# One 64x64 burst for the next chunk's scores and this chunk's output, and state matmuls in bursts of their own

## The chip, the cores and the metric

The kernel runs on 1 core of one Trainium2 chip. The metric is device microseconds of one execution; most executions of one kernel agree within 0.3%. Comparisons are between executions with a granted TensorE clock of 0.99 or more.

## The reference, cut to what matters

Two attention layers on the same 2048 x 1024 input, each with 32 heads of 32 columns. A is linear attention, B looks at 8 earlier positions, two apart. A gate g mixes them.

```python
def _A_ref(x, wqkv, wo):                 # linear attention
    q, k, v = ...                        # x @ wqkv, split in heads
    pq, pk = phi(q), phi(k)
    kv  = einsum("bhsd,bhse->bhde", pk, v)        # the "state", 32 x 32 a head
    z   = einsum("bhsd->bhd", pk)
    num = einsum("bhqd,bhde->bhqe", pq, kv)
    den = einsum("bhqd,bhd->bhq", pq, z)[..., None] + 1e-6
    return (num / den) ... @ wo

def _B_ref(x, wqkv, wo):                 # window of W = 8 positions, dilation 2
    logits = einsum("bhsd,bhswd->bhsw", q, kg) * scale
    attn   = softmax(where(mask, logits, -1e9))
    return einsum("bhsw,bhswd->bhsd", attn, vg) ... @ wo

g = sigmoid((x * gate_w).sum(-1, keepdims=True))
return g * _A_ref(...) + (1 - g) * _B_ref(...)
```

## The kernel before

The work is nearly all dense 128x128 matmuls over 512 columns (the projections). Between them stand short bursts of small ones:

- **S**, scores of B for one chunk of queries: 32 matmuls on 64x64 tiles of the array;
- **PV**, the output of B for a chunk, token-major: 64 matmuls with 64 rows and 57 columns of weights, also on the 64x64 grid;
- **kv**, the state of A for two tiles of 128 tokens: 64 matmuls with 128 rows and 32 columns of weights.

There are 18 chunks and 16 token tiles. The four PSUM banks `SO` hold scores, and later the values of the same chunk; `main` has the other four, for dense groups and for the state. The first burst after all of these is called fold: it multiplies the state into A's output weights.

```python
def s_fn(e):                                     # S: 32 matmuls into all four SO banks
    for c in range(8):
        for h in range(2):
            for r in range(2):
                last = e.matmul(SO[2 * r + c // 4]..., kT[64 * r:..., c, ...], Q[64 * r:..., c, ...],
                                tile_position=(64 * r, 64 * h))
# ...
def rest(...):
    P.op("pe", s_fn, ..., writes=[s.iv for s in SO], name="S")        # a burst of its own
    # E = exp(scores) on ScalarE from the four SO banks, then the mask on VectorE
    def values():
        def each(e):                             # PV: 64 matmuls, back into the four SO banks
            for i in range(16):
                for w in range(2):
                    for h in range(2):
                        last = e.matmul(SO[2 * h + i // 8]..., E[64 * h:..., ...], vt[64 * h:..., ...],
                                        tile_position=(64 * h, 64 * w))
        fns = [each]
        if len(states) > 1 and states[1][0] <= slot_n[0]:
            fn, more, bank, add = state([states.pop(0)[1] for _ in range(2)])
            fns = fns + [fn]                     # kv of two token tiles behind the values
        P.op("pe", lambda e: [f(e) for f in fns][-1], ..., name="PV" if add is None else "PV+kv")
        # two reciprocals and two multiplies on VectorE, then the output's DMAs
    after(PVLAG, values)
# ...
def state(two):
    bank = main.next()
    def fn(e):                                   # kv: 8 x 2 x 4 matmuls, 128 rows x 32 columns
        for s in range(8):
            for i, (t, pkt, azt) in enumerate(two):
                for c in range(4):
                    last = e.matmul(bank.ap()[32 * c:32 * c + 32, ...], pkt[...], azt[:, h, :],
                                    start=(i == 0), stop=(i == len(two) - 1), tile_position=(0, 32 * c))
    def add():                                   # VectorE adds the bank to kva and so frees it
```

Of the kernel before, what the change touches and what calls it, by code (L numbers as in the profile page):

```python
# [7 lines left out]
ALU = mybir.AluOpType  # L8
AX = mybir.AxisListType
BF16 = mybir.dt.bfloat16  # L10
F32 = mybir.dt.float32
# [1105 lines left out]
def build_kernel(nc, A_x, A_wqkv, A_wo, B_x, B_wqkv, B_wo, gate_w, out):  # L1117
# [86 lines left out]
    ot = Ring([SB([128, 1024], BF16, "ot%d" % i) for i in range(2)])  # L1204
    rs = Ring([SB([128, 16], F32, "rs%d" % i) for i in range(4)])
    vr = Ring([SB([128, 33 * H], BF16, "v%d" % i) for i in range(2)])
# [22 lines left out]
    FILL = 0.2  # L1229
    PVLAG = 3  # L1230
    WARM = 11
    PASSES = 6
# [4 lines left out]
    def plan(seen):  # L1237
# [6 lines left out]
        class Pool:  # L1244
# [4 lines left out]

            def next(self):  # L1250
                if seen is None:
                    b = self.bs[self.n % len(self.bs)]
                else:
                    b = min((b for b in self.bs if b.take is None or b.take in P.read), key=lambda b: seen[b.take] if b.take is not None else -1.0)
                self.n += 1
                b.take = len(takes)
                takes.append(len(P.ops))
                return b

        for b in banks:  # L1260
            b.take = None

        def C(eng, fn, cost, writes, reads=()):
# [34 lines left out]
        def top_end(i, op):  # L1298
            P.op("dve", lambda e: e.tensor_reduce(mx4[:, i:i + 1], mx[i][:, :], AX.X, op), 0.15 + mx[i].row / 960.0, reads=[mx[i].all()], writes=[mx4.part((i, i + 1))])

# [117 lines left out]
        def fill(e_, qs, nq, offs):  # L1418
# [7 lines left out]

            Q, _ = qd.next()
            for k in range(2):
                src = qT[:, :, t0 + qs:t0 + qs + 2 * nq]
                fd = lambda e, k=k: e.tensor_scalar(Q[:, :, k, 0:2 * nq], src, par[:, k:k + 1], None, op0=ALU.mult)  # L1430
                fa = lambda e, k=k: e.activation(Q[:, :, k, 0:2 * nq], src, ACT.Copy, scale=par[:, k:k + 1])
                P.op("any", {"act": fa, "dve": fd}, {"act": act(16 * nq), "dve": 0.15 + 16 * nq / 1920.0}, reads=[qT.part((0, 8), (t0 + qs, t0 + qs + 2 * nq)), par.all()],
                     writes=[Q.part((0, 8), (k, k + 1), (0, 114))])

# [10 lines left out]
        def rest(e_, qs, nq, t0, k0, m, vt, Q, s_fn):  # L1445
            P.op("pe", s_fn, 0.46, mode="r", reads=[kT.part((0, 8), (t0 + k0[0], t0 + k0[1] + 64)), Q.all()], writes=[s.iv for s in SO], name="S")
            E, _ = Er.next()
# [3 lines left out]
            P.op("dve", lambda e: e.tensor_tensor(ev(), ev(), m[:, :, :].rearrange("p r q -> p (r q)")[:, None, :].to_broadcast([128, 16, 2 * nq]), ALU.mult),  # L1451
                 0.15 + 32 * nq / 1920.0, reads=[E.all(), m.all()], writes=[E.all()])

            def values():

                def each(e):
                    for i in range(16):
                        for w in range(2):
                            hd = 16 * w + i
                            for h in range(2):  # L1460
                                c = 33 * (i % 8)
                                g_ = place(hd)
                                last = e.matmul(SO[2 * h + i // 8].ap(c, c + 33)[64 * w:64 * w + nq, :], E[64 * h:64 * h + 64, g_ * nq:(g_ + 1) * nq],  # L1463
                                                vt[64 * h:64 * h + 64, hd * 33:hd * 33 + 33], start=True, stop=True, tile_position=(64 * h, 64 * w))
                    return last
                fns, rd, wr, add = [each], [vt.all(), E.all()], [s.iv for s in SO], None
                if len(states) > 1 and states[1][0] <= slot_n[0]:
                    fn, more, bank, add = state([states.pop(0)[1] for _ in range(2)])
                    fns, rd, wr = fns + [fn], rd + more, wr + [bank.iv]
                P.op("pe", lambda e: [f(e) for f in fns][-1], 0.55 + 0.5 * (len(fns) - 1), mode="c", reads=rd, writes=wr, name="PV" if add is None else "PV+kv")  # L1470
                if add is not None:
                    add()
                o, os_ = ot.next()
                for h in range(2):
                    r, _ = rs.next()
                    bv = lambda h=h: ps[:, 4 + 2 * h:6 + 2 * h, 0:264].rearrange("p k (i c) -> p k i c", c=33)
                    two = [SO[2 * h].iv, SO[2 * h + 1].iv]
                    P.op("dve", lambda e, r=r, bv=bv: e.reciprocal(r[:, :].rearrange("p (k i) -> p k i", k=2), bv()[:, :, :, 32:33].rearrange("p k i c -> p k (i c)")), 0.2,
                         reads=two, writes=[r.all()])
                    P.op("dve", lambda e, r=r, bv=bv, h=h: e.tensor_tensor(  # L1480
                        o[:, 512 * h:512 * h + 512].rearrange("p (k i c) -> p k i c", k=2, c=32), bv()[:, :, :, 0:32],
                        r[:, :].rearrange("p (k i) -> p k i", k=2)[:, :, :, None].to_broadcast([128, 2, 8, 32]), ALU.mult), dps(512),
                        reads=two + [r.all()], writes=[o.part((512 * h, 512 * h + 512))])
                q0 = t0 + qs
                for w, (r0, r1) in [(w, r_) for w in range(2) for r_ in ((0, 48), (48, nq))]:
                    P.op("sp", lambda e, w=w, r0=r0, r1=r1: e.dma_start(
                        oB_hbm[q0:q0 + 2 * nq, 512 * w:512 * w + 512].rearrange("(h q) f -> q h f", h=2)[r0:r1], o[64 * w + r0:64 * w + r1, :].rearrange("p (h f) -> p h f", h=2)), 0.5,
                        reads=[o.all()], writes=[[("O%d_%d" % (w, r0), q0, q0 + 2 * nq, None)]], chan="oo%d_%d_%d" % (os_, w, r0), lat=0.3)
                while rows[0] < NT and q0 + 2 * nq >= 128 * (rows[0] + 1):
                    t, rows[0] = rows[0], rows[0] + 1  # L1490
                    P.op("sp", lambda e, t=t: e.dma_start_transpose(qT[:, :, t * 128:(t + 1) * 128], oB_hbm[t * 128:(t + 1) * 128, :]), 1.5,
                         reads=[[("O%d_%d" % (w, r0), t * 128, (t + 1) * 128, None)] for w in range(2) for r0 in (0, 48)], writes=[qT.part((0, 8), (t * 128, (t + 1) * 128))], chan="ot%d" % t, lat=1.3)
            after(PVLAG, values)

        rows = [0]
        pace = [0.0]

        states = []

        def slot(rate):  # L1500
            slot_n[0] += 1
            while later and later[0][0] <= slot_n[0]:
                later.pop(0)[1]()
            if len(states) > 1 and states[1][0] + 2 <= slot_n[0] and not later:
                fn, rd, bank, add = state([states.pop(0)[1] for _ in range(2)])
                P.op("pe", fn, 0.42, mode="c", reads=rd, writes=[bank.iv], name="kv")
                add()
            pace[0] = min(pace[0] + rate, 1.0) if todo else 0.0
# [39 lines left out]
        def state(two):  # L1548
# [17 lines left out]
            return fn, [x.all() for _, p, a in two for x in (p, a)], bank, add  # L1566

        for t in range(NT):
            pkt, _ = pk.next()
            azt, _ = az.next()  # L1570
            xs, xr = x_tile(t)
            for r in range(4):
                bank = main.next()
                w, wr = w_half((3, 0)[r // 2], r % 2)
# [9 lines left out]
                if r == 3:  # L1584
                    states.append((slot_n[0] + 1, (t, pkt, azt)))
                slot(FILL)
        while todo or later or states:
            slot(1.0)
        load_w(3, 0, Bo, 0, 50)
# [3 lines left out]

        P.op("dve", lambda e: e.tensor_reduce(mx4[:, 3:4], kva[:, :, 32:33], AX.XY, ALU.max), 0.2, reads=[kva.all()], writes=[mx4.part((3, 4))], prio=1e5)
        P.op("dve", lambda e: e.tensor_copy(kvb[:, :, :], kva[:, :, 0:32]), 0.35, reads=[kva.all()], writes=[kvb.all()])
        P.op("dve", lambda e: e.transpose(kvT[:, :], kvb[:, :, :].rearrange("p s d -> p (s d)")), 0.4, reads=[kvb.all()], writes=[kvT.all()])
        for c in range(4):
            for r in range(4):
                k = 4 * (c % 2) + r
                P.op("dve", lambda e, c=c, r=r, k=k: e.tensor_copy(zsel[32 * r:32 * r + 32, c:8:4, k:k + 1], kva[32 * c:32 * c + 32, r:8:4, 32:33]), 0.16,  # L1600
                     reads=[kva.all()], writes=[zsel.all()], prio=1000 + len(P.ops) + 100)

# [105 lines left out]
        for n, (u, j) in enumerate(nums):  # L1708
# [3 lines left out]
            slot(0)  # L1712
            if n in (3, 5, 7, 9):
                fold((n - 3) // 4, (n - 3) // 2 % 2)
            if n >= 20:
# [102 lines left out]
```

## Time and profile before

| | before |
|---|---|
| time, median of 3 executions | 486.6 us (486.26 to 486.74) |
| span of the profiled execution | 485.2 us, granted clock 1.0 |
| first scores burst to first fold burst (the stretch with all S, PV and kv bursts) | 189.80 us |
| the dense matmul's pitch, from start to start | 0.2158 us |

The views and lines that carry the bound are in the prediction below. One more view is the timeline of the weight loads (columns: start in us, length, engine, line, operation, output and input, shapes, count, and in brackets the idle time just before). The trace has 4403 loads, one before each matmul, and some matmul records are missing (4339), so loads are counted, from start to start; that also avoids the ends of the matmuls, which the profile models. One pair of bursts in the stage of the q and k projections, kernel before:

```profile
149.54 0.45 PEld L1440 LDWEIGHTS ps_all<-qd,kT 64*64 64x64 bf16 x32 [0.42 <-DVE mx L1295]
150.07 4.86 PEld L1334 LDWEIGHTS ps_all<-xT,w 128*128 128x128 bf16 x24
155.36 0.58 PEld L1463 LDWEIGHTS ps_all<-v,E 64*57 64x57 bf16 x64 [0.42 <-DVE mx L1295]
155.97 3.14 PEld L1334 LDWEIGHTS ps_all<-xT,w 128*128 128x128 bf16 x16
159.53 0.45 PEld L1440 LDWEIGHTS ps_all<-qd,kT 64*64 64x64 bf16 x32 [0.42 <-issue]
```

S takes 0.53 us to the next dense load, PV 0.61, and the whole period is 159.53 - 149.54 = 9.99 us. The 40 dense matmuls of the period are 40 x 0.2158 = 8.63; with the two bursts, 1.14, that leaves 0.22.

The second view is where the stretch begins and ends:

```profile
129.56 0.45 PEld L1440 LDWEIGHTS ps_all<-qd,kT 64*64 64x64 bf16 x32 [0.42 <-issue]
...
319.36 0.14 PEld L1610 LDWEIGHTS ps_all<-w,kvT 32*32 32x32 bf16 x16 [0.42 <-DVE e L1345]
```

From the first scores load to the first fold load it is 189.80 us. All that the change moves lies in between.

### The profile page before, as it was taken

To read this page: it belongs to the slowest core of one execution; us is meant where nothing else is said; L and a number is where in the kernel's file an instruction comes from. 1 tells how busy PE (TensorE), PEld (TensorE's weight loads), DVE (VectorE), ACT (ScalarE), POOL (GpSimd) and SP (SyncE) were. 2 spreads that over 40 slices of the span, in tenths; PEclk is the share of its full clock that TensorE was granted. 3 is DMA by queue.
4 is the path that set the end of the run, shared out by engine and by line. 5 is a ranking of instruction groups with operands and counts; after the bars stand their busy time and mean duration, and the time that the engine had idled before them with its cause. 6 is when DMAs were issued, how large, how long until landed. Compare 5 with 4: busy or idle time off the path is not lost.

```text
span 485.2 us, 10105 instructions
## 1 busy us (share of the span) xinstructions
PE 474.2 (98%) x4339; PEld 222.8 (46%) x4403; DVE 285.2 (59%) x547; ACT 140.2 (29%) x227; POOL 5.9 (1%) x36
## 2 busy tenths in 40 slices
PE   8999999999999999999999999999999999999997
PEld 3444444444444444454544554444444444444443
DVE  2121435888688888665666556496579236653434
ACT  2111121235322234334443333455532230111000
POOL 4000000000000000000000000000000000000000
PEclk9999999999999999999999999999999999999999
DMA  8999993132014459433222322820086018830212
GB/s 224 222 194 299 309 355 122 65 110 86 1 44 135 107 138 245 100 76 86 55 75 67 85 66 66 204 54 2 10 217 163 1 15 242 221 24 2 88 68 89
DMA packets 72951, 57.39 MB, mean 118 GB/s; under 512 B 37953, under 2 KB 60865, under 8 KB 72898
## 3 DMA queue, kind: packets, MB, share of 16 engines
q1 hardware_dynamic: 72210, 56.07, 44.3%
q8 instruction: 36, 0.59, 0.5%
q10 hardware_dynamic: 688, 0.59, 0.4%
q14 instruction: 17, 0.14, 0.1%
HBM read 34.49 MB, written 13.76 MB: 99 GB/s over the span
## 4 chain that ended last, share of the span: by engine, by line
PE 95%; SPq 2%; issue 1%; DMA 1%; ACT 0%; DVE 0%
PE ps_all L1334 78%; PE ps_all L1693 11%; PE ps_all L1463 2%; PE ps_all L1440 2%; SPq L1308 1%; DMA w<-in_B_wqkv_dram 1%; PE ps_all L1556 1%; SPq L1313 1%; PE ps_all L1638 0%; PE ps_all L1610 0%; ACT e L1341 0%; DVE o L1697 0%
## 5 line engine op out<-in xcount | busy, mean ns | idle before, releaser
L1334 PE MATMUL ps_all<-w,xT 128*128 128x512 bf16 x924 | 208.6, 379 | 4.5 <-issue 2.1
L1334 PE MATMUL ps_all<-xT,w 128*128 128x512 bf16 x745 | 166.3, 379 | 2.2 <-issue 1.4
L1334 PEld LDWEIGHTS ps_all<-w,xT 128*128 128x128 bf16 x960 | 91.2, 98 | 111.1 <-DMA w<-in_B_wqkv_dram 2.1
L1334 PEld LDWEIGHTS ps_all<-xT,w 128*128 128x128 bf16 x768 | 73.9, 98 | 88.7 <-issue 1.3
L1693 PE MATMUL ps_all<-w,qT 128*128 128x512 bf16 (+1 forms) x260 | 55.4, 372 | 0.2
L1693 PEld LDWEIGHTS ps_all<-w,qT 128*128 128x128 bf16 x264 | 25.9, 98 | 29.6
L1365 DVE CAST vst<-ps_all 128x512 bf16<-128x512 f32 x15 | 10.4, 694 | 43.5 <-PE ps_all L1334 43.5
L1448 ACT ACTIVATE E<-ps_all 128x1824 bf16<-128x1824 f32 (+1 forms) x18 | 30.4, 1689 | 13.4 <-PE ps_all L1440 13.4
L1345 DVE TENSOR_SCALAR e<-e 128x512 bf16<-128x512 bf16 x64 | 18.4, 290 | 26.9 <-ACT e L1343 14.0
L1697 DVE SCALAR_TENSOR_TENSOR o<-ps_all,gm,xT 128x512 bf16<-128x512 f32 (+1 forms) x25 | 18.0, 728 | 21.1 <-PE ps_all L1693 20.8
L1341 ACT ACTIVATE e<-ps_all 128x512 bf16<-128x512 f32 x32 | 19.1, 598 | 39.0 <-PE ps_all L1334 38.1
L1343 ACT ACTIVATE e<-ps_all 128x512 bf16<-128x512 f32 x32 | 19.1, 598 | 32.3 <-PE ps_all L1334 32.3
L1295 DVE TENSOR_TENSOR mx<-mx,kT 128x1024 bf16<-128x1024 bf16 x32 | 20.9, 688 | 10.9 <-ACT kT L1366 10.8
L1295 DVE TENSOR_TENSOR mx<-mx,qT 128x1024 bf16<-128x1024 bf16 x32 | 20.8, 687 | 7.9 <-ACT qT L1369 7.9
L1451 DVE TENSOR_TENSOR E<-E,msk 128x1824 bf16<-128x1824 bf16 (+1 forms) x18 | 19.9, 1104 | 7.8 <-ACT E L1448 7.4
L1366 ACT ACTIVATE vst<-ps_all 128x512 bf16<-128x512 f32 x17 | 10.2, 601 | 48.5 <-PE ps_all L1334 45.1
L1480 DVE TENSOR_TENSOR ot<-ps_all,rs 128x512 bf16<-128x512 f32 x36 | 23.3, 686 | 0.0
L1366 ACT ACTIVATE az<-ps_all 128x512 bf16<-128x512 f32 x22 | 13.2, 601 | 34.5 <-PE ps_all L1334 34.5
L1366 ACT ACTIVATE kT<-ps_all 128x512 bf16<-128x512 f32 x20 | 11.9, 597 | 37.6 <-PE ps_all L1334 37.6
L1347 DVE SCALAR_TENSOR_TENSOR pk<-ps_all,e 128x512 bf16<-128x512 f32 x32 | 22.0, 689 | 0.7
L1369 ACT ACTIVATE qT<-ps_all 128x512 bf16<-128x512 f32 x19 | 11.4, 598 | 37.4 <-PE ps_all L1334 37.3
L1369 ACT ACTIVATE xT<-ps_all,g 128x512 bf16<-128x512 f32 x10 | 6.9, 689 | 45.1 <-PE ps_all L1334 45.1
(72 smaller groups left out, 260.2 us busy)
## 6 DMA issues: line engine op xcount, KB each, us to landing
rb<-rc_hbm SPq DMA_DIRECT2D x32, 256.0 KB, 5.2
w<-in_A_wqkv_dram SPq DMA_DIRECT2D x6, 1024.0 KB, 9.0
v<-vB_hbm SPq DMA_DIRECT2D x36, 132.0 KB, 2.7
vB_hbm<-vst SPq DMA_DIRECT2D x32, 132.0 KB, 6.2
w<-in_B_wqkv_dram SPq DMA_DIRECT2D x4, 1024.0 KB, 9.5
xn<-in_A_x_dram SPq DMA_DIRECT2D x16, 256.0 KB, 2.7
out_dram<-o SPq DMA_DIRECT2D x15, 256.0 KB, 2.1
oB_hbm<-ot SPq DMA_DIRECT2D x36, 96.0 KB, 2.2
```

The source lines that it names most:

```text
L1295: P.op("dve", lambda e, m=m, op=op: e.tensor_tensor(m[:, 0:n], m[:, 0:n], src, op), 0.08 + n / 1920.0, reads=[m.all(), reg], writes=[m.all()],
L1334: last = e.matmul(bank.ap(), lhs(dc), rhs(dc), start=(dc == 0), stop=(dc == 7))
L1341: P.op("act", lambda e: e.activation(e_[:, :], bank.ap(), ACT.Exp), act(512), reads=[bank.iv], writes=[e_.all()])
L1343: P.op("act", lambda e: e.activation(e_[:, :], bank.ap(), ACT.Exp, accum_out=qe[:, col:col + 1]), act(512) + 0.1, reads=[bank.iv], writes= ...
L1345: P.op("dve", lambda e: e.tensor_scalar(e_[:, :], e_[:, :], 1.0, 1e-6, op0=ALU.min, op1=ALU.add), 0.25, reads=[e_.all()], writes=[e_.all()])
L1347: P.op("dve", lambda e: e.scalar_tensor_tensor(out=dst, in0=bank.ap(), scalar=0.0, in1=e_[:, :], op0=ALU.max, op1=ALU.add), dps(512), read ...
L1366: fa = lambda e: e.activation(dst, src(), ACT.Copy)
L1369: fa = lambda e: e.activation(dst, src(), ACT.Copy, scale=scale)
L1448: P.op("act", lambda e: e.activation(E[:, 0:32 * nq].rearrange("p (j q) -> p j q", j=4), ps[:, 4:8, 0:8 * nq], ACT.Exp), act(32 * nq), rea ...
L1451: P.op("dve", lambda e: e.tensor_tensor(ev(), ev(), m[:, :, :].rearrange("p r q -> p (r q)")[:, None, :].to_broadcast([128, 16, 2 * nq]), ...
L1480: P.op("dve", lambda e, r=r, bv=bv, h=h: e.tensor_tensor(o[:, 512 * h:512 * h + 512].rearrange("p (k i c) -> p k i c", k=2, c=32), bv()[:, ...
L1693: last = e.matmul(bank.ap(0, f1 - f0), qT[:, dc, t * 128:(t + 1) * 128], ws[3][:, dc, f0:f1], start=(dc == 0), stop=(dc == 7))
```

## The change

Its intent: S of the next chunk and PV of this chunk are the same kind of work for TensorE (64x64 tiles), so they become one burst, and two changes of tiling are saved. For that the values can't go into the score banks, which the same burst writes: 15 of 16 head pairs go to two `main` banks, and the sixteenth to a free corner of two score banks. The state, which has another shape, gets bursts of its own between dense groups.

```diff
-            P.op("pe", s_fn, 0.46, mode="r", ..., writes=[s.iv for s in SO], name="S")
+            claim(SO[3])
+            evac = None
+            if pend:
+                evac = pend.pop()(s_fn, s_reads)          # the values of the chunk before, scores ahead of them
+            else:
+                P.op("pe", s_fn, 0.46, mode="c", ..., writes=[s.iv for s in SO], name="S")
 ... exp, mask (mask with a later priority: MASKLAG) ...
+            if evac is not None:
+                evac()
-            def values():
+            def values(s_fn=None, s_reads=()):
+                two = [main.next() for _ in range(2)]
                 def each(e):
+                    if s_fn is not None:
+                        s_fn(e)
                     for i in range(16):
 ...
-                                c = 33 * (i % 8)
+                                bk, c = (two[h], 33 * i) if i < 15 else (SO[1 + h], 456)
 ...
-                if len(states) > 1 and states[1][0] <= slot_n[0]:
-                    fn, more, bank, add = state(...)
-                    fns, rd, wr = fns + [fn], rd + more, wr + [bank.iv]
-                P.op("pe", lambda e: [f(e) for f in fns][-1], ..., name="PV" if add is None else "PV+kv")
+                P.op("pe", each, 1.0 if s_fn else 0.55, ..., writes=[b.iv for b in SO + two], name="S+PV" if s_fn else "PV")
 ...
-                for h in range(2):                        # reciprocal and multiply, twice
+                for h, n in ((0, 15), (1, 15), (2, 1)):   # and a third, small pair
 ...
+        def run_state():
+            fn, rd, bank, add = state([states.pop(0)[1] for _ in range(2)])
+            P.op("pe", fn, 0.55, mode="k", ..., name="kv")
 ...
-                bank = main.next()
+                bank = main.next([SO[3]] if r == 2 else [])   # may lend a score bank to a dense group
-                slot(FILL)
+                slot(1.0 if r == 1 and t % 4 < 3 else 0.0)
+                if r == KVAT and t % 2 and t > 1:
+                    run_state()
 ... (cut: max/min reductions halved by tensor-tensors first, queries held behind the last
      multiply, fold bursts two dense groups later)
```

## The prediction

> **What bounds the kernel now.** I read the page's busy times and its chain that ended last, then the waits of the matmul engine, then its timeline, a burst at a time.
>
> ```profile
> PE 474.2 (98%) x4339; PEld 222.8 (46%) x4403; DVE 285.2 (59%) x547; ACT 140.2 (29%) x227; POOL 5.9 (1%) x36
> ...
> PE 95%; SPq 2%; issue 1%; DMA 1%; ACT 0%; DVE 0%
> ```
>
> The chain is TensorE for 95% of the span, at a granted clock of 9 tenths or more in every slice of the page. What lies outside is the head (15.3 us until the chain reaches the first long matmul stretch) and some 3 us at the end; the change touches neither. VectorE at 59% and ScalarE at 29% only matter if they make TensorE wait. The waits of TensorE:
>
> ```profile
> PE ps_all L1334 <- issue: 3.5, 22, 0.2
> PE ps_all L1373 <- DVE warm L1283: 1.3, 1, 1.3
> PE ps_all L1334 <- DMA xT<-in_A_x_dram: 0.6, 2, 0.3
> PE ps_all L1334 <- DMA w<-in_B_wqkv_dram: 0.5, 2, 0.3
> PE ps_all L1334 <- ACT e L1341: 0.2, 1, 0.2
> ```
>
> Nothing here is a wait for a bank or for VectorE that a better order could remove. The 22 waits for "issue" look like a cost at the end of each burst, but the timeline says otherwise (a values burst, "PV"):
>
> ```profile
> 185.32 0.58 PEld L1463 LDWEIGHTS ps_all<-v,E 64*57 64x57 bf16 x64 [0.42 <-DVE mx L1299]
> ...
> 185.93 4.86 PEld L1334 LDWEIGHTS ps_all<-w,xT 128*128 128x128 bf16 x24
> ...
> 186.16 5.13 PE L1334 MATMUL ps_all<-w,xT 128*128 128x512 bf16 x23 [0.16 <-issue]
> ```
>
> After a values burst the trace has one record fewer of dense matmuls than of weight loads (x23 against x24), and the first weight load comes 0.11 us after the last small matmul (185.32 + 0.50, worked out below, = 185.82). So the first matmul after the burst is a missing record, not a pause of 0.16 us. The same holds for the single 0.16 us put down to ACT e. In truth TensorE waits for nothing from 15.3 us to the end: the time is dense matmuls at 0.2158 us each (50 in 10.79 us), plus the bursts of small matmuls, and only what a burst costs can be won.
>
> **What a burst costs.** One scores burst ("S") and one kv state burst appended to a values burst:
>
> ```profile
> 148.80 0.81 PE L1334 MATMUL ps_all<-xT,w 128*128 128x512 bf16 x3
> 149.54 0.60 PE L1440 MATMUL ps_all<-qd,kT 64*64 64x114 bf16 x32
> 150.07 0.60 PE L1334 MATMUL ps_all<-xT,w 128*128 128x512 bf16 x2
> ```
>
> ```profile
> 215.87 0.68 PE L1463 MATMUL ps_all<-v,E 64*56 64x33 bf16 x64
> 216.48 0.67 PE L1556 MATMUL ps_all<-az,pk 128*32 128x33 bf16 x64
> 217.30 0.81 PE L1334 MATMUL ps_all<-w,xT 128*128 128x512 bf16 x3 [0.16 <-issue]
> ```
>
> From start to start (the start of a group's last matmul is the group's start, plus its length, less one matmul's duration: 379, 208, 178 or 184 ns):
> - dense to S: 149.54 - (148.80 + 0.81 - 0.379) = 0.31, that is 0.093 over the pitch of 0.216;
> - inside S: 0.60 - 0.208 = 0.392 for 31 steps, 12.6 ns a matmul;
> - S to dense: 150.07 - (149.54 + 0.392) = 0.138;
> - inside PV: 0.68 - 0.178 = 0.50 for 63 steps, 8 ns; PV to dense 0.108;
> - PV to kv: 216.48 - (215.87 + 0.50) = 0.108; inside kv 0.486; kv to dense (the load at 217.07) 0.104.
>
> A check without the trace's modelled ends: from S at 149.54 to PV at 155.36 there are 24 dense matmuls, 5.82 - 5.18 = 0.64 for S; from PV to the next S 16, 4.17 - 3.45 = 0.72 for PV. So the pair costs 1.36 us, of which 0.43 or so is four switches of about 0.1. A kv burst costs 0.59 appended (216.48 to 217.07), and standing alone (at 313.48, next dense load 314.07, entry 0.093) 0.68: one switch more.
>
> [...] every change of shape costs about 0.1 us, while inside S or PV, which walk over four 64x64 tiles, matmuls start 8 to 13 ns apart. Scores have 64 rows and 64 columns of weights, values 64 rows and 57 columns: both stand on the 64x64 grid, and both walk the four tiles in the same order. The state burst is 128x32, another mode. [...]
>
> **The change, part by part.** The order of TensorE's instructions in the built kernel after:
> 1. Before: 18 S visits, 11 PV, 7 PV+kv, 1 kv. After: 1 S, 17 S+PV, 1 PV, 8 kv. The six fold and den bursts stay, and so do all dense matmuls and all small ones.
> 2. 17 merges. Each takes out S-to-dense (0.138) and dense-to-PV (0.093), 0.231, and puts in the step from the last score to the first value. In one tiling mode that is a step of 10 to 40 ns; I take 0.02. Saved: 17 x 0.21 = 3.6 us.
> 3. 7 kv bursts set apart: each puts PV-to-dense and dense-to-kv in place of PV-to-kv, one switch more, 0.093. Lost: 7 x 0.093 = 0.65 us.
> 4. VectorE per chunk, before: two reciprocals (226 ns) and two multiplies (686 ns), 1.8 us. After: the same two pairs a little smaller (15 heads of 16), plus a pair on 2 heads, which I estimate at 0.2 + 0.2 us from the reciprocal row and from VectorE's rows on 16 and 32 elements a partition (0.17 to 0.25 us). 18 x 0.3 = 5.4 us more on an engine that has 200 us to spare: off the path. The two reductions over 1024 (1212 ns each) become three halvings and a reduction over 128; at 688 ns for a 1024-wide tensor-tensor that is about 0.4 + 0.25 + 0.2 + 0.25, hardly less, in four pieces that others can slip between. No gain on the path, as TensorE doesn't wait there.
> 5. The output now takes two of the four dense banks per burst. Their release is the one new wait that could matter; see rival 2. I allow 0.3 us in all.
>
> Sum: -3.6 + 0.65 + 0.3 = -2.6 us on 486.6: 484.0 us.
>
> **The rivals.**
> 1. *Scores and values are not one mode for the hardware* [...]. Then a merge saves only 0.231 - 0.108 = 0.12: 17 x 0.12 = 2.1, less 0.65: 485.2 us. For it: PV to kv costs a full switch even between small matmuls. Against: that pair differs in rows and columns, and within S the tiles alternate freely.
> 2. *A bank wait takes the switch's place.* A burst of 1.1 us is followed by a dense group every 1.73 us. The first two groups use the two remaining banks; the third starts 3.5 us after the burst and needs one of the two output banks, free after latency, two reciprocals and a multiply (0.2 + 0.36 + 0.65 = 1.2 us), or 2.5 us when VectorE has just begun its two max and min operations (1.29 us). VectorE is busy 47.3 of 56.4 us in the stretch 129.6 to 186 and 72.0 of 118 from 196 to 314, so it is tight only in the first. If each of 17 bursts lost 0.2 us: 487.4 us. Likewise the merged burst needs scores' queries and masked exponentials ready together; in the second stretch queries wait for the last multiply, which waits for exponential (1.69) and mask (1.1): some 5.5 us of the 6.9 us between bursts. Plausible for a few bursts, not for all.
> 3. *Merged bursts delay the exponential by 0.6 us*, as it now waits for the last value matmul. The values come a whole period (8.6 us) later, so it is hidden.
>
> **Range and chances.** Rival 1 gives 485.2, the full saving without any wait 483.6; waits of up to 2 us on the main sum 485.8. I take 483.0 to 486.0 for 8 in 10. Either way is far below 2% (9.7 us): the two kinds of burst together cost 18 x 1.36 + 8 x 0.6 = 29 us, nearly all of it matmuls that stay. Faster by over 2%: 0.01; within: 0.98; slower: 0.01.
>
> **What would show it.** In the trace after: S and the values burst follow each other with a step of under 40 ns between last score and first value (right) or about 0.1 us (rival 1); merged burst, from first score to the next dense weight load, 1.02 to 1.05 us against rival 1's 1.11; kv bursts alone with 0.1 us at both ends; the span of the chunk stretch shorter by some 2.6 us, the dense stretches before and after unchanged. Waits of TensorE on DVE rs or ot rows, or on ACT, longer than the 0.16 us of a missing record, would show rival 2. The prediction is wrong if dense matmuls start more than 0.22 us apart around the bursts, or if the stage's length changes by anything other than switches.

The 0.231, 0.093 and 0.108 are the starts in its own list; the 0.108 in rival 1 is the step from PV to kv. The 0.02 us (10 to 40 ns) for the step from score to value is the author's estimate; in the trace before, the steps between the loads of one scores burst are 0 to 45 ns. The 0.2 us of latency in rival 2 is an estimate too; there a reciprocal that waits for the values starts 0.26 us after the last value matmul's start.

## The result

| | before | after |
|---|---|---|
| median of 6 executions | 486.68 us (486.26 to 487.17) | 484.06 us (483.86 to 484.62) |
| ratio after / before | | 0.9947, 95% interval 0.9934 to 0.996 |
| span of the profiled execution, clock | 485.2 us, 1.0 | 482.1 us, 1.0 |
| first scores burst to first fold | 189.80 us | 190.75 us; less 16 dense matmuls moved into it 187.30 |

A ratio here and below is the mean time of one kernel's fast executions over that of the other's of the same rounds, so not quite the ratio of the medians quoted. The change gains 2.6 us, 0.5%: within 2%, and with an interval that excludes no change.

The page of the kernel after has, for busy times and for the chain that ended last:

```profile
PE 472.3 (98%) x4349; PEld 224.3 (47%) x4403; DVE 280.3 (58%) x578; ACT 149.3 (31%) x238; POOL 5.8 (1%) x36
...
PE 95%; DVE 2%; ACT 1%; issue 1%
```

The bound is the same: TensorE, 95% of the chain, with the same 4403 weight loads. Its waits, in the list of waits (columns: who, for whom, us in total, times, longest):

```profile
PE ps_all L1343 <- issue: 3.8, 24, 0.2
...
PE ps_all L1343 <- DVE pk L1356: 0.6, 4, 0.2
```

Apart from the warm-up's 1.3 us at the head, which the dots leave out, none is longer than 0.2 us. The four put down to VectorE's `pk` are again the 0.16 us of a missing matmul record: behind the state burst at 222.01 the dense weight load starts on time at 222.61, and only the first dense matmul's record is lacking.

The same stretch of weight loads as shown of before:

```profile
148.14 0.45 PEld L1450 LDWEIGHTS ps_all<-qd,kT 64*64 64x64 bf16 x32 [0.42 <-issue]
148.53 0.62 PEld L1485 LDWEIGHTS ps_all<-v,E 64*57 64x57 bf16 x64
149.18 8.31 PEld L1343 LDWEIGHTS ps_all<-xT,w 128*128 128x128 bf16 x40
157.91 0.45 PEld L1450 LDWEIGHTS ps_all<-qd,kT 64*64 64x64 bf16 x32 [0.42 <-issue]
```

Scores run into values without a pause: 0.39 us from the first scores load to the first values load, which is what the 32 scores themselves take, and 0.65 from there to the dense load. The burst is 1.04 us where the two apart took 0.53 + 0.61 and one entry more. The period is 9.77 us, against 9.99: 0.21 to 0.22 us less for each merge. A state burst standing alone:

```profile
208.08 0.57 PEld L1579 LDWEIGHTS ps_all<-az,pk 128*32 128x32 bf16 x64 [0.42 <-DVE ot L1502]
208.68 8.31 PEld L1343 LDWEIGHTS ps_all<-w,xT 128*128 128x128 bf16 x40
```

It takes 0.60 us plus an entry of 0.11. And the ends of the stretch:

```profile
129.09 0.45 PEld L1450 LDWEIGHTS ps_all<-qd,kT 64*64 64x64 bf16 x32 [0.42 <-issue]
...
319.84 0.14 PEld L1646 LDWEIGHTS ps_all<-w,kvT 32*32 32x32 bf16 x16 [0.42 <-DVE zsel L1636]
```

That is 190.75 us, 0.95 more than before, but the first fold now stands 16 dense matmuls later (3.45 us): 187.30, or -2.50. From the first fold load to the last weight load of the program the two kernels agree once those 16 are counted (162.61 us, and 159.16 + 3.45). The rest of the difference between the two spans, 0.47 us, is the head, where the first scores burst starts at 129.56 and 129.09; among the runs with an untouched head it starts anywhere from 129.1 to 130.0, also where no edit differs there, so that part is scatter.

Where the 2.50 us come from, counted over the trace: 17 merges at 0.21 are -3.57. Seven more state visits at 0.107 are +0.75. Four of the 17 merged bursts have one small hiccup among their values (0.68 to 0.76 us in place of 0.65), +0.30 in all. The sum is -2.52. Every dense stretch in between runs at its pitch in both kernels.

### The profile page after: what moved, and what is told of

It is laid out like the page before. It is cut to its first block, busy times and chain, and to the rows that moved or that the text cites. A ratio compares the mean times of both kernels' runs of the same rounds, so it can differ in the third digit from the quotient of the medians.

```text
span 482.1 us, 10165 instructions
## 1 busy us (share of the span) xinstructions
PE 472.3 (98%) x4349; PEld 224.3 (47%) x4403; DVE 280.3 (58%) x578; ACT 149.3 (31%) x238; POOL 5.8 (1%) x36
## 4 chain that ended last, share of the span: by engine, by line
PE 95%; DVE 2%; ACT 1%; issue 1%
PE ps_all L1343 77%; PE ps_all L1729 11%; PE ps_all L1485 2%; PE ps_all L1450 2%; ACT E L1464 1%; PE ps_all L1382 1%; DVE E L1467 1%; DVE pk L1356 1%; PE ps_all L1579 0%; PE ps_all L1674 0%; DVE qd L1440 0%; PE ps_all L1646 0%; DVE e L1354 0%; DVE rs L1501 0%; DVE ot L1502 0%
## 5 line engine op out<-in xcount | busy, mean ns | idle before, releaser
L1343 PEld LDWEIGHTS ps_all<-w,xT 128*128 128x128 bf16 x960 | 92.3, 98 | 110.1 <-issue 1.6
L1502 DVE TENSOR_TENSOR ot<-ps_all,rs 128x480 bf16<-128x480 f32 (+1 forms) x54 | 25.8, 505 | 0.0
L1375 ACT ACTIVATE az<-ps_all 128x512 bf16<-128x512 f32 x24 | 14.4, 599 | 36.2 <-PE ps_all L1343 36.2
L1501 DVE RECIPROCAL rs<-ps_all 128x15 f32<-128x15 f32 (+1 forms) x54 | 9.4, 203 | 27.8 <-PE ps_all L1485 25.9
```

Source lines behind the costliest of these rows:

```text
L1343: last = e.matmul(bank.ap(), lhs(dc), rhs(dc), start=(dc == 0), stop=(dc == 7))
L1375: fa = lambda e: e.activation(dst, src(), ACT.Copy)
L1502: P.op("dve", lambda e, r=r, src=src, dst=dst, m=m: e.tensor_tensor(dst, src()[:, :, 0:32], r[:, 0:m, None].to_broadcast([128, m, 32]), AL ...
```

## The experiments

Twelve kernels ran. "Stretch" is first scores load to first fold load in the profiled execution, 190.75 us in the kernel after. The ratio is to the kernel before in the same call, whose median was 486.8 us in the first two calls, 486.95 in the third and 486.56 in the last.

| run | edit | median us (range, n) | ratio, 95% | stretch us |
|---|---|---|---|---|
| e1_switch | after, one 128x32 matmul between S and PV | 487.93 (487.64 to 488.26, 5) | 1.0022, 1.0008 to 1.0035 | 194.30 |
| e2_same | after, one 64x64 matmul there | 484.39 (484.01 to 484.8, 5) | 0.9952, 0.9939 to 0.9966 | 190.77 |
| e3_kv_alone | before, kv taken out of PV | 487.71 (487.4 to 487.83, 5) | 1.0018, 1.0004 to 1.0031 | 190.48 (before: 189.80) |
| e4_kv_appended | after, kv behind S+PV | 489.39 (488.88 to 489.93, 5) | 1.005, 1.0036 to 1.0064 | 196.14 |
| e6_dve_order | after, VectorE's order as before | 484.09 (483.95 to 484.16, 5) | 0.9944, 0.993 to 0.9957 | 190.62 |
| e10_no_third_bank | kv ahead of S+PV in an output bank, wrong result | 488.83 (488.26 to 489.53, 5) | 1.0044, 1.003 to 1.0058 | 195.53 |
| e9_kv_four | after, kv of four token tiles | 484.63 (484.56 to 485.72, 5) | 0.996, 0.9946 to 0.9973 | 191.42 |
| e11_four_lend | the same, fourth score bank lent | 485.23 (484.61 to 485.89, 5) | 0.9965, 0.9952 to 0.9979 | 191.14 |
| e12_four_shift | e9, program shifted by 52 loads | 491.14 (484.47 to 492.34, 6, two of them slow; the four fast ones 490.5) | 1.0046, 1.0003 to 1.0089 | 189.82 |
| e13_after_shift | after, shifted the same | 489.29 (485.3 to 492.43, 6) | 1.0031, 0.9995 to 1.0067 | 190.69 |
| e14_four_split | e9, last kv burst in two | 484.75 (484.63 to 485.22, 5) | 0.9956, 0.9943 to 0.9969 | 191.18 |
| e15_four_warm | e9, shifted by 55 loads, 66 short warm-up matmuls | 490.23 (486.9 to 491.96, 6) | 1.0062, 1.0037 to 1.0086 | 189.88 |

### Is it the change of shape? e1_switch and e2_same

Theory: the gain is the two changes of shape that each merge saves. Rival: it is something else about having one burst rather than two, such as fewer separate operations. One extra matmul is put between scores and values in the 17 merged bursts, once with another shape, once with the same one. What it writes is overwritten by the values of the same burst, so both results stay correct.

```diff
                     if s_fn is not None:
                         s_fn(e)
+                        # e1: 128 rows x 32 columns          e2: 64 rows x 64 columns
+                        e.matmul(two[0].ap(0, 33)[0:32, :], kT[:, 0, ... +32], kT[:, 1, ... +33], ...)
```

> The kernel after, with one extra 128x32 matmul of 33 columns between the scores and the values of each of the 17 merged bursts (its output lands in an output bank and is overwritten, so results stay right). Theory (the gain is the number of changes of tile grid on TensorE): the step of 0.043 us from scores to values becomes two switches of 0.10 to 0.14 us, +0.20 us a burst, 17 x 0.20 = +3.3 us: about 487.4 us, the whole gain gone. Rival (the gain came from banks, queues or VectorE's order, which this leaves as they are): at most 17 x 0.01, about 484.2 us.

> The control of the run above: the extra matmul is 64x64, on the grid of its neighbours. Theory: one step of about 0.01 us more a burst, 17 x 0.01 = 0.2 us: 484.2 us. If it came out near 487, one more matmul or one more read or write would be the cost in the other run, and not the switch.

The weight loads of e1, then of e2:

```profile
158.90 0.45 PEld L1450 LDWEIGHTS ps_all<-qd,kT 64*64 64x64 bf16 x32 [0.42 <-issue]
159.43 0.09 PEld L1479 LDWEIGHTS ps_all<-kT 128*32 128x32 bf16 x1
159.56 0.58 PEld L1486 LDWEIGHTS ps_all<-v,E 64*57 64x57 bf16 x64
160.17 8.31 PEld L1343 LDWEIGHTS ps_all<-xT,w 128*128 128x128 bf16 x40
```

```profile
157.98 0.45 PEld L1450 LDWEIGHTS ps_all<-qd,kT 64*64 64x64 bf16 x32 [0.42 <-issue]
158.37 0.10 PEld L1479 LDWEIGHTS ps_all<-kT 64*64 64x64 bf16 x1
...
159.04 8.32 PEld L1343 LDWEIGHTS ps_all<-xT,w 128*128 128x128 bf16 x40
```

With the other shape the burst is 160.17 - 158.90 = 1.27 us, with the same shape 1.06. The scores now take 0.53 us to the next load's start, as they did in front of dense work, and the single 128x32 matmul takes 0.13 where a 64x64 one takes 0.02 (a burst of 1.06 against 1.04 without it). The two stretches differ by 194.30 - 190.77 = 3.53 us, 0.208 a burst, and the times by 3.5 us. One small matmul of the wrong shape takes back all that a merge gives. This confirms the first half of the change, by shape and not by count: the rival, that fewer operations matter, would have made e1 and e2 alike.

### What a state visit costs: e3_kv_alone

In the kernel before, the state is taken out of the values burst and left to stand alone; besides this, only the planner's cost and mode for the state operation are changed.

```diff
-                if len(states) > 1 and states[1][0] <= slot_n[0]:
+                if False:
...
+            burst = False
             while later and later[0][0] <= slot_n[0]:
+                burst = True
                 later.pop(0)[1]()
-            if len(states) > 1 and states[1][0] + 2 <= slot_n[0] and not later:
+            if len(states) > 1 and states[1][0] + 2 <= slot_n[0] and not burst:
...
```

> The second half of the change alone: the kernel before, scores and values still apart, with the state matmuls in bursts of their own (7 of 8 alone, 1 still behind a scores burst; before it was 1 of 8). Theory: 6 switches more at 0.107 us, +0.64 us: 487.3 us against 486.7. Rival (setting the state bursts apart relieves something and is part of the gain): below 486.5 us.

Seven visits were set apart, one of which fell behind a scores burst, so there are six switches more. The stretch grew by 0.68 us, 0.113 a switch, and the time by 0.9 us, 0.4 more than expected; the spans of the profiled executions, 485.9 against 485.2, agree with the stretch. The second half of the change, taken by itself, is a loss. Why is it there then?

### Putting the state back: e4_kv_appended and e10_no_third_bank

The obvious better kernel keeps the merge and appends the state to it: seven visits fewer, 0.75 us less.

```diff
+                fns, more, wr, add = [each], [], [b.iv for b in SO + two], None
+                if s_fn is not None and len(states) >= 2 and states[1][0] <= slot_n[0]:
+                    fn, more, bank, add = state([states.pop(0)[1] for _ in range(2)])
+                    fns, wr = fns + [fn], wr + [bank.iv]
+                P.op("pe", lambda e: [f(e) for f in fns][-1], ...)
...
-                if r == KVAT and t % 2 and t > 1:
-                    run_state()
```

> The first half alone: the kernel after with 7 of the 8 state bursts appended to a merged burst, as the kernel before appended them to a values burst. Theory of switches alone: 7 fewer at 0.107 us, -0.75 us: 483.3 us, faster than both kernels. Rival (the state bursts stand apart because a merged burst with them takes three of the four dense banks and TensorE then waits for one): waits of TensorE on VectorE or ScalarE of 0.2 to 0.6 us in each of the 7, 484.7 to 487.5 us.

It is slower, by 5 us. The switch theory alone missed this by 6 us. Its waits and a piece of its weight loads:

```profile
PE ps_all L1343 <- issue: 5.0, 17, 1.7
PE ps_all L1343 <- DVE kva L1597: 3.1, 3, 1.0
```

```profile
196.50 1.19 PEld L1343 LDWEIGHTS ps_all<-w,xT 128*128 128x128 bf16 x7
199.72 4.19 PEld L1343 LDWEIGHTS ps_all<-w,xT 128*128 128x128 bf16 x20 [2.03 <-issue]
```

There are two different losses. One was on record as the rival: a burst with three outputs takes three of the four `main` banks, and the dense group behind it waits until VectorE has added the state to `kva`. That is 3 times 0.86 us of delay in the loads, plus 0.85 us once before a burst, where a cast held a bank: 3.4 us. The other was on nobody's list: twice TensorE stood still for 2.13 and 1.49 us from load to load (1.9 and 1.07 us more than the normal steps there) with nothing released at the end of it; the profile says "issue". In the first case it stops before the eighth load of a dense group, whose bank had been its own for seven matmuls. The sum, -0.75 + 3.4 + 3.0 = 5.65, is near the 5.39 by which the stretch grew.

I first took the third bank to be the cause of both. To test it, the state was put ahead of the scores into the first output bank, so that the burst takes only two banks. The values then overwrite the state before it is added: the result is wrong (relative error 0.103), the time is what counts.

```diff
+                    fn, more, bank, add = state([states.pop(0)[1] for _ in range(2)], two[0])
+                    fns = [fn] + fns
```

> Wrong results on purpose: as the run with the appended state bursts, but the state matmuls go ahead of the scores into the first output bank, where the values overwrite them, so that the merged burst takes two dense banks and not three. Same number of switches, same instructions. If the third bank is what cost the appended kernel 6 us of waits: 483.3 to 485.0 us. If it is the longer burst, or the addition of the states among VectorE's evacuations, that costs: 486.5 us or more.

The waits for `kva` and for the cast are gone, as they should be, yet the time is 488.83 us, in the range that was to show the third bank not to be the main cause. What remains is the other loss, and larger:

```profile
PE ps_all L1485 <- issue: 2.6, 1, 2.6
```

It is inside a values burst, before its last weight load, at 199.69 us. Behind it eight dense matmuls run at 0.43 us apiece, half the pace of 0.2158; the profiled execution's mean granted clock is 0.996. What slows them no run here was made to tell. So my explanation by banks was half of it at best.

### VectorE's order and the lent bank: e6_dve_order and a build that wasn't run

The remaining parts of the change are the reductions in halves, the mask's later priority and the queries held behind the last multiply. All three were undone.

```diff
-    MASKLAG = 12
+    MASKLAG = 0
...   tensor_reduce over all 1024 again, in place of three tensor-tensors and one over 128
-            held = last_evac[-1:]
+            held = []
```

> The kernel after without its three rules for VectorE: the two reductions over 1024 elements again in one piece each, the mask at its old priority, the query copies no longer held behind the last evacuation. Theory (TensorE waits for nothing in either kernel, so VectorE's order is off the path): within 0.3 us of the kernel after, 484.1 us. Rival (part of the gain is VectorE's order): 484.6 us or more, with waits of TensorE on VectorE in the trace.

484.09 us against 484.06: inert, as expected. The lending of a score bank to a dense group is inert too, and that could be seen without a run: built without it, the program comes out identical, as the plan that is chosen never takes up the offer. A run would have shown nothing.

### Fewer, longer state bursts: e9_kv_four and e11_four_lend

If a visit costs 0.1 us twice over, four token tiles a visit save four visits. Two more buffers of each kind were needed, placed in a weight buffer whose later rows are then loaded later.

```diff
-            fn, rd, bank, add = state([states.pop(0)[1] for _ in range(2)])
+            fn, rd, bank, add = state([states.pop(0)[1] for _ in range(4)])
-                if r == KVAT and t % 2 and t > 1:
+                if r == KVAT and t % 4 == 1 and t > 1:
```

> A version meant to beat both: the kernel after with the state matmuls of four token tiles in one burst, 4 state bursts in place of 8, still standing apart and with one bank each. The two more buffers that this needs lie in the part of a weight buffer whose load is put off until they are free. Theory: 4 visits fewer, each saving an entry and an exit of about 0.1 us, 4 x 0.19 = 0.76 us: 483.3 us. If a late weight load or a bank takes its place: 484 us or more, with a wait of TensorE on that load or bank.

> The same, and the third dense group of each token tile always uses the fourth scores bank, which the kernel after only allows and, by its order, never does. Theory: dense groups wait for no bank already, so nothing moves: 483.3 us, the same as without. Rival (banks are short): faster by 0.3 us or more than the run without.

Both missed: 484.63 and 485.23 us, no better than the kernel after. The last state burst of e9:

```profile
311.52 0.96 PEld L1581 LDWEIGHTS ps_all<-az,pk 128*32 128x32 bf16 x112 [0.42 <-issue]
313.87 0.17 PEld L1581 LDWEIGHTS ps_all<-az,pk 128*32 128x32 bf16 x16 [1.39 <-issue]
314.08 1.84 PEld L1345 LDWEIGHTS ps_all<-xT,w 128*128 128x128 bf16 x10
```

It stops after 112 of its 128 loads for 1.4 us. No data can be missing there: the 16 loads left read the same token tiles as those before them. In e11 the same stop lasts 1.3 us. Here the question could be put: what does TensorE wait for when it waits for nothing that the profile shows?

### Finding the stop

I counted weight loads from the start of the program. The stops of different kernels come at the same count, at times that differ by microseconds, and the counts lie a whole number of about 127.6 loads apart. And each comes 1.3 to 1.5 us after a packet on the DMA queue that the page calls "instruction":

```
kernel                        weight load no.   packet landed at   stop ended at   from load to load
e4_kv_appended                     1618             198.40             199.72          2.13
e10_no_third_bank                  1618             198.25             199.69          2.77
e4_kv_appended                     2511             255.66             257.04          1.49
e10_no_third_bank                  2511             255.94             257.39          1.31
e9_kv_four                         3531             312.36             313.87          1.48
e11_four_lend                      3531             312.49             313.88          1.27
e10_no_third_bank                  3532             316.23             317.52          0.51
e14_four_split (below)             3532             310.12             311.59          1.05
2511 - 1618 = 893 = 7 x 127.6      3532 - 2511 = 1021 = 8 x 127.6      (times in us)
```

On the page of the kernel after, the queue reads (packets, MB, share):

```profile
q8 instruction: 36, 0.59, 0.5%
```

0.59 MB in 36 packets is 16 KB each, and 4403 loads with their matmuls over 36 packets are 122 pairs a packet, near the 127.6 between the stops. So I take one packet to bring one block of TensorE's program, 127.6 pairs long. What a packet holds the profile doesn't say. A pair of dense matmul and load lasts 0.2158 us, so a block lasts 27.5 us of dense work; a state burst goes through 128 pairs in 1.1 us (e12), and one packet alone takes 0.9 to 2.4 us in these five kernels (0.88 to 2.12 in the kernel after).

That TensorE stops to wait for such a block is a theory drawn from counts. It has a sharp consequence: the stop belongs to a place in the program, not to the burst. Move the program by nearly half a block and the stop must leave the place in the burst where it was.

### Moving the program: e12_four_shift, e13_after_shift, e14_four_split, e15_four_warm

e12 puts 60 tiny matmuls at the start of e9 in place of 8 of the 11 warm-up matmuls (52 loads more); e13 does the same to the kernel after, as a control. e14 leaves the program's place alone and splits the last state burst in two of 64. e15, the last run, mends e12's slow head (figures below): 66 warm-up matmuls of 86 columns in place of 11 of 512 (55 loads more), with the same order of instructions as e9 on every engine.

```diff
 e12, e13
-    WARM = 11
+    WARM = 3
+        P.op("pe", lambda e: [e.matmul(banks[7].ap(0, 8), warm[:, 0:128], warm[:, 0:8], ...) for _ in range(60)][-1], ...)
 e14
+                if r == KVAT and t == 15:
+                    run_state(2)           # and 2 more at the end, in place of 4
 e15
-            P.op("pe", lambda e: e.matmul(banks[7].ap(), warm[:, 0:128], warm[:, :], ...), 0.43, ...)
+            P.op("pe", lambda e: [e.matmul(banks[7].ap(0, 86), warm[:, 0:128], warm[:, 0:86], ...) for _ in range(6)][-1], 0.43, ...)
```

> The kernel with four token tiles per state burst again, with 60 tiny matmuls put at the start in place of 8 of the 11 warm-up matmuls, so that TensorE's instruction stream is shifted by 60 weight loads [...]. Theory (TensorE waited for its program in the last state burst): the stall of 1.3 to 1.5 us in the last state burst is gone or much smaller, and the time is 483.0 to 483.6 us, about 1.2 us under the unshifted one's 484.63. Rival (the stall belongs to the burst's data or to the transfers of that moment): the stall stays at the same burst and the time stays at 484.4 to 484.9 us. If the theory holds but the shift lays the end of another block into another burst, a stall of about the same size is found at a weight-load index that is again a multiple of about 127.5 away from 1618, 2511 and 3531.

> Control: the changed kernel with the same shift of 60 weight loads and 3 warm-up matmuls. Both theories: no burst is longer than 96 matmuls, so no stall comes or goes: 484.1 +- 0.4 us. What differs from the changed kernel's 484.06 is the price of the shift at the head, and is to be taken off the shifted four-tile kernel too.

> Four token tiles per state burst, but the last state burst split in two of 64 matmuls: five state bursts in place of the changed kernel's eight, so 3 visits fewer, 3 x 0.19 to 0.21 us = 0.6 us: 483.5 us. Theory (program feed): the burst of 128 matmuls was too long for the feed at that place, two of 64 with dense work between them are not: no stall over 0.5 us, 483.3 to 483.8 us. Rival (the data or the transfers of that moment): the stall appears in one of the two halves, 484.6 to 485.2 us.

> The kernel with four token tiles per state burst, with only its 11 warm-up matmuls of 512 columns replaced by 66 of 86 columns: [...] the same order of instructions on every engine, but TensorE's program is shifted by 55 weight loads. Theory (TensorE waited for a block of its program in the last state burst): no stall over 0.4 us in any burst, first scores burst to first fold about 189.8 us as in the shifted run before it (191.42 unshifted), and 483.1 us in all (482.8 to 483.5), which would be the fastest version: 0.9965 to 0.998 of the changed kernel's time. Rival (the stall belongs to the burst's data or transfers): the last state burst takes 2.5 us again and the time is 484.6. If the late output transfer of the two shifted kernels came from the shift itself [...], it shows again as a wait of VectorE for out_dram in the last stage, and the time is 486 or more.

The last state burst of e15, to be laid beside that of e9:

```profile
312.03 1.19 PEld L1581 LDWEIGHTS ps_all<-az,pk 128*32 128x32 bf16 x128 [0.42 <-issue]
313.25 2.70 PEld L1345 LDWEIGHTS ps_all<-xT,w 128*128 128x128 bf16 x14
```

All 128 loads in one run, 1.22 us to the dense load in place of 2.56. In e12 it is 1.13 us. Neither has a stop over 0.1 us in any burst. The stretch is 189.82 us in e12 and 189.88 in e15 against 191.42 in e9 (e15's expectation had said 189.8), and 190.69 in the shifted control: four visits fewer are worth 0.87 us, near the 4 x 0.2 that had been expected of e9 from the start. The order of loads on TensorE and of instructions on VectorE and ScalarE is the same in the traces of e9, e12 and e15. In this stretch, with one profiled execution of each, the theory's consequence is confirmed: the stop of e9 goes when the program is moved. The rival, that it belongs to the burst's data or to transfers of that moment, is refuted. The end of the block itself, load 3532, still lies in this burst, only earlier (after 61 of its loads in e12, after 58 in e15); by the count it is passed 3.3 to 3.4 us after its packet has landed, where the stops come after 1.3 to 1.5.

e14 tells where my wording was too narrow. I had expected that a burst of 64 matmuls with dense work around it doesn't stop. It did:

```profile
310.12 0.51 PEld L1581 LDWEIGHTS ps_all<-az,pk 128*32 128x32 bf16 x57 [0.42 <-DVE ot L1504]
311.59 0.12 PEld L1581 LDWEIGHTS ps_all<-az,pk 128*32 128x32 bf16 x7 [0.95 <-issue]
```

The stop is at load 3532 again, in one of the two halves, and the time of 484.75 us lies in the range put down for the rival: by its letter this expectation failed. What counts isn't the length of one burst: here 64 values, 8 dense and 57 state pairs went by in some 3 us before the stop. Nor is it speed alone: the 128 loads before the stops of e9 and e11 and the last one of e10 took 4.5 to 6.2 us, and in e4 and e10 the 128 loads before load 3022 went by in 1.3 us without a stop.

What all stops share is the packet. Take the packets in order, one for every 127.6 loads, from load 1618 on and back. Of the 322 blocks so counted between loads 600 and 3600 in all 14 traces, none begins sooner than 1.30 us after its packet has landed. Nine begin after 1.30 to 1.51 us: the eight stops of the table and a delay of 0.08 us in e4. All others come after 1.62 us or more. So every stop seen here goes with a packet that lands late for its block. Packets start when 0 to 149 loads are left before their block, 103 in the middle; for the two stops at load 1618 it was 2 and 0.

The block nearest to a stop without having one is in the kernel after, which passes load 3532 too, in a state burst, 1.62 us after its packet has landed (310.96, by the same count), where the stops end 1.3 to 1.5 us after. By these figures, an estimate, it gets through with 0.1 to 0.3 us to spare.

The times of the shifted kernels are another matter, and three expectations failed there. They were to be 483.0 to 483.6, 484.1 and 483.1 us, and came out at 491.1 (490.5 for its fast executions), 489.3 and 490.2, with a wide scatter (e12's fastest execution had 484.47, the control's 485.30; two of e12's six, the profiled one among them, count as slow, at a mean clock of 0.993 and 0.997). The stretch readings above are from before the place where this scatter arises, with dense matmuls at their pitch (in e15 the 32 behind the last state burst take 7.08 us; 31 pitches and one matmul's 0.38 are 7.07). In e12 and e13 a part is the head: the first scores burst starts at 131.08 and 130.81 us against 129.09 to 129.97 without the shift; e15 has 130.38. In e12 the first 36 dense matmuls take 9.91 us, where 35 pitches and 0.38 are 7.93; in e15 an early group of 28 of them, at 8.34 us, takes 6.22 against 6.21. The larger part comes in the last stage. Waits of e15, and its TensorE timeline there:

```profile
PE ps_all L1345 <- DVE o L1738: 4.4, 1, 4.4
```

```profile
428.93 20.34 PE L1345 MATMUL ps_all<-w,xT 128*128 128x512 bf16 x80 [4.40 <-DVE o L1738]
```

VectorE waits 6.4 us for an output transfer to free a buffer, TensorE 4.4 us for VectorE, and the 80 matmuls then take 20.34 us in place of 17.4 (79 pitches and one matmul's 0.38), as 14 of them stand 0.43 us apart, at half the pace; the execution's mean granted clock is 0.992. The control has the same wait (4.9 us), so it goes with the shift and not with the state bursts; e15 has it with early matmuls at their pitch, so it doesn't come from the slow ones at e12's head. Slow packets alone don't tell the kernels apart: at that time they take up to 5.03 us in e15, but up to 4.7 in e9 and 5.4 in the kernel after too, where VectorE waits 2.6 and 2.5 us at most for such a buffer and TensorE not at all. Why the output transfer comes late in the three shifted kernels, in their profiled executions and by the times in most of the others, stays open; the runs were used up. So no version that beats the kernel after was found, though one is 0.9 us faster in the stretch that the change is about.

## Why the prediction was right

The median of 484.06 us lies within 0.1 us of the predicted 484.0. By its own steps:

1. **The bound and the visits.** Right. TensorE is the chain in both kernels, and the visits are those counted: 1 S, 17 S+PV, 1 PV, 8 kv.
2. **17 merges at 0.21 us.** Right, and shown twice: by the period (9.77 us against 9.99) and by e1, where one matmul of another shape takes back 3.53 us in 17 bursts. Two terms in it were off and cancelled. The entry from dense work costs 0.107 us, not 0.093; and the step from the last score's load to the first value's is 38 to 44 ns, not 20, at the edge of the "under 40 ns" that was to show the prediction right. It is a step that scores take among themselves too (108 of the 558 steps inside the scores bursts of the kernel after are 37 to 45 ns), and far from the 0.1 us of the rival.
3. **Seven state visits at 0.093 us.** Right in kind; the size was 0.107, so 0.75 in place of 0.65 us. e3 measured it apart at 0.113.
4. **VectorE's extra work is off the path.** Right: no wait for it over 0.2 us is in the list, and when e6 undid VectorE's order nothing changed.
5. **0.3 us for bank waits.** Right in size by luck, wrong in kind. No bank wait is seen. The 0.30 us are four hiccups of 0.03 to 0.11 us inside merged bursts, whose cause I have not found.
6. **Rival 1** (from scores to values costs a full switch) fell: e2's extra 64x64 matmul cost 0.02 us a burst, e1's 128x32 one 0.21 us more than that. **Rival 2** (bank waits) did not come in this kernel, but it was no empty worry: it came as soon as a burst had a third output (e4, 3.4 us). **Rival 3** (the later exponential) is hidden; no wait of TensorE on the exponential is in the list.

What the prediction did not see is what the state's separate bursts are good for. It booked them as a loss of 0.65 us. e3 confirms the loss, but e4 shows that the alternative costs 5 us: 3.4 us for the third bank, and 3.0 us in two stops behind bursts of 160 small matmuls, which I put down to TensorE waiting for its own program. That last cause is shown as far as this: the stops stay at the same places of the program in five kernels, they end 1.3 to 1.5 us after a 16 KB packet of the instruction queue, and the one of e9 goes when the program is moved. For the stops of e4 and e10 the program was not moved; they are put down to the same cause by their place and their packet. What decides when a packet is asked for, and what the 1.4 us after its landing are, stays open.

## What to carry to other kernels

Put bursts of small matmuls that share a tiling mode together: each change between the shapes of this kernel cost 0.09 to 0.14 us on TensorE, also between two small ones (0.11 from values to state). Read such costs from the starts of weight loads, not from matmul ends or from "issue" waits of 0.16 us, which here were missing records (24 and 4 such waits in the kernel after, while its weight loads show no pause there). Before lengthening a burst of small matmuls, count: here one 16 KB packet of the instruction queue came for every 127.6 weight loads, a burst of 128 went by in 1.1 to 1.2 us (e12, e15), and none of the 322 blocks so counted began sooner than 1.30 us after its packet had landed. A stop of this kind reads as an "issue" wait, at the same weight-load count in different kernels (1618, 2511 and 3531 or 3532). Some 50 loads added far ahead removed one here, but those kernels lost 5 us or more elsewhere.
